# A new order for the first slots of a sparse-attention and feed-forward kernel, with 18 filler matmuls

## The chip, the cores and the metric

The kernel runs on one core of a Trainium2 chip. The metric is device microseconds of one execution. An execution of the kernel took 270.89 us (median of three, 269.55 to 270.93).

## The reference

Attention with two sparse masks, then a multiplicative feed-forward network on its output. B = 8, 8 heads, 576 rows, head width 64; 4608 tokens, model width 512, inner width 1024.

```python
scores = scale * np.matmul(q, k.transpose(0, 1, 3, 2))
mask_local = (rel >= 0) & (rel < stride)                   # heads 0..3, stride 32
mask_strided = (rel >= 0) & (pos[None, :] % stride == pos[:, None] % stride)   # heads 4..7
scores = np.where(masks, scores, -1000000000.0)
scores = scores - np.max(scores, axis=-1, keepdims=True)
attn = np.exp(scores)
attn = attn / (np.sum(attn, axis=-1, keepdims=True) + 1e-09)
x = np.matmul(attn, v)                                     # as 4608 tokens x 512
out = ((x @ w1) * (x @ w2) @ w3) @ w_out
```

## The kernel before

The work is cut into 32 *pairs*: pair i is two heads of batch i // 4. Pairs with i % 4 = 0 or 1 are local, 2 or 3 strided. The steps of a pair, with their lines:

- `load_qk` (L88): q and k from HBM to the tile `s16` (four buffers), cast to fp16 on the way, issued on GpSimd's queue: one transfer each for a local pair (L100), two each for a strided one (L105).
- `load_v` (L108): a local pair's v goes as fp32 in small pieces to one of two tiles `vsL`, three transfers on SyncE's queue (L117, L119); with `gate` a memset on VectorE comes first (L115). A strided pair's v goes as fp16 to `vhS`, four transfers on GpSimd's queue (L130).
- `emit_T` (L292): 36 or 44 transposes on TensorE (L301) into the two buffers of the PSUM pool `psA`, and the copies of q and k out of it (L309 local, L314 and L315 strided).
- `emit_S` (L319): the scores on TensorE (L333 local, L339 strided) and the addition of the mask on VectorE (L345).
- `emit_max` (L353), `emit_sub` (L360) on VectorE, `emit_exp` on ScalarE (L372), `emit_norm`: sum and reciprocal on VectorE (L380, L382), the product on GpSimd or, with `dve`, on VectorE (L383).
- `emit_P`: five or six transposes of the probabilities (L401), through `psA` too, and one copy (L404).
- `emit_cast_v` (L281): a local pair's v to fp16; `shift_v` (L289, L290): a copy of it moved by 32 rows, by two transfers on SyncE's queue.
- `emit_V`: probabilities times v (L421 local, L438 strided), copied to `xT` (L426, L442, L444, L446).

The weights w3 and w_out are folded into one matrix `wfh`. `load_w3` (L212) loads two blocks of w3 as one transfer of 512 KB (of the fp16 written), `load_wo` (L208) half of w_out, `load_w` (L205) half of w1 or w2, all on GpSimd's queue. `fold_t` (L223, L225) makes eight transposes and a copy, `fold_m` (L233, L236) four 128x512 matmuls for each of two halves and, after the second, a copy to `wfh`. The default engine of a copy in `fold_m`, `emit_P` and `emit_V` is ScalarE, in `fold_t` VectorE, in `emit_cast_v` GpSimd; in the order, `cp` is VectorE and `act` ScalarE.

The feed-forward part runs over nine chunks of 512 tokens. A piece of it is `emit_a` (L248, L252) or `emit_b` (L258, L261): four 128x512 matmuls each, a copy on ScalarE, a product on VectorE; sixteen such pieces make a chunk, then `emit_out` (L269, L274, L275) eight matmuls for each of four blocks of rows. `feed(us, batches)` emits pieces, 0.87 for one of a or b and 1.74 for an output block, until its credit is used up; nothing can be fed before x of the first 512 tokens, that is V of pairs 0 to 3, is there.

All PSUM tiles but those of `psA` come from one pool of six buffers (`psF`). Every engine works through its instructions in the order of emission, as the five queues have it. That order is written out by hand as a list of steps for the first slots, up to pair 8 or so (L504 to L674 before); then a loop (L675) goes on for pairs 9 to 31, and `feed(1e9, B)` ends it. GpSimd's transfers use eight semaphores in turn: each issue waits for the landing of the one eight issues before it. Where GpSimd's queue holds a product of `emit_norm`, all issues behind it wait as well.

`warm(n)` (L485) is n matmuls 128x512 of a zeroed tile `wz` into a `psF` buffer that nobody reads. It is defined before the change, but not called.

The stretch of the list before that matters here, shortened:

```python
zero_S(); load_v(1); load_qk(0, "k"); make_maskL(); load_qk(1, "k"); make_identity(nc, id16)
load_qk(0, "q"); load_qk(1, "q"); load_v(0, True); load_w3(2, 2)
```

Of the kernel before, what the change touches and what calls it, by code (L numbers as in the profile page):

```python
# [27 lines left out]
def kernel(  # L28
# [79 lines left out]
    def load_v(i, gate=False):  # L108

        b, hp, local, par = where(i)  # L110
        h0 = 2 * hp
        if local:
            vt = vsL[par]
            if gate:
                nc.vector.memset(vt[:, 0:LC - 1, 0, 0:1], 0.0)  # L115
            for h in range(2):
                nc.sync.dma_start(vt[:, 0:LC - 1, h, :],  # L117
                                  _ap(v[b, h0 + h], 0, [[D, P], [P * D, LC - 1], [1, D]]))
            nc.sync.dma_start(vt[0:HALF, LC - 1],  # L119
                              v[b, h0:h0 + 2, P * (LC - 1):S].rearrange("h p d -> p h d"))  # L120
        else:
            vt = att.tile([P, 2, 6 * D], FP16, tag="vhS", bufs=4, name="vhS")
            if i + 1 == 4 * B:
                nc.vector.memset(vt[HALF + 32:P, 1, 4 * D:5 * D], 0.0)
            for half in range(2):
                for h in range(2):
                    n = 6 - half
                    for r0, ap, m in strided_rows(i, h, n):
                        m = m if half else n
                        nc.gpsimd.dma_start(vt[HALF * half + r0[0]:HALF * half + r0[1], h, 0:m * D],  # L130
                                            _ap(v[b, h0 + h], 6 * half * D + ap[0],
                                                ap[1] + [[1, m * D]]))
            pts.setdefault(i, {})["v"] = vt.rearrange("p h (t d) -> p t h d", d=D)
            return
        staged[i] = vt
# [23 lines left out]
    def make_sel():  # L159
        nc.gpsimd.memset(sel, 1.0)  # L160
        for sg in (1, -1):
            nc.gpsimd.affine_select(out=sel, in_=sel, compare_op=ALU.is_ge, fill=0.0, base=0,
                                    pattern=[[0, 22], [sg, 3]], channel_multiplier=-sg)
# [43 lines left out]
    def load_wo(c):  # L207
        nc.gpsimd.dma_start(woh[:, c:c + 4, :], wor[:, c:c + 4, :])  # L208

    def load_w3(c, n=2):  # L210
        w3 = wst.tile([P, n, DF], FP16, tag="w3s", bufs=4, name="w3s")
        nc.gpsimd.dma_start(w3.rearrange("p i n -> p (i n)"), w3r[:, c // 2, :])  # L212
        for i in range(n):
            w3st[c + i] = w3[:, i, :]
# [276 lines left out]
    def zero_S():  # L491
        for t in qTS + prS:
            nc.vector.memset(t, 0.0)
# [7 lines left out]
    dve = nc.vector  # L501
    cp, act, pool = nc.vector.tensor_copy, nc.scalar.copy, nc.gpsimd.tensor_copy
    with tc.manual_schedule():
        zero_S()  # L504
        load_v(1)
        load_qk(0, "k")
        make_maskL()
        load_qk(1, "k")
        make_identity(nc, id16)
        load_qk(0, "q")  # L510
        load_qk(1, "q")
        load_v(0, True)
        load_w3(2, 2)
        load_qk(2, "k")
        load_qk(2, "q")
        make_sel()
        load_wo(0)
        load_qk(3, "k")
        zero_L(1)
        zero_L(0)  # L520
        emit_T(0, cp)
        load_w3(0, 2)
        emit_S(0)
        emit_T(1)
        load_qk(3, "q")
        emit_max(0)
        emit_cast_v(1, cp)
        nc.vector.memset(wz, 0.0)
        load_wo(4)
        make_maskS()  # L530
        load_v(3)
        emit_sub(0)
        emit_exp(0)
        emit_norm(0)
        emit_S(1)
        emit_T(2)
        fold_t(3, act)
        fold_t(2, act)
        emit_cast_v(0, cp)
        emit_max(1)  # L540
        load_w3(4, 2)
        emit_sub(1)
        load_qk(4, "k")
        emit_exp(1)
        fold_m(3, 0)
        load_qk(4, "q")
        fold_m(2, 0)
        emit_S(2)
        emit_norm(1)
        shift_v(0)  # L550
        emit_T(3)
        load_w(w1r, w1h, 0)
        load_v(2)
        fold_t(0, cp)
        fold_t(1, act)
        emit_P(0)
        emit_S(3)
        emit_max(3)
        load_w(w2r, w2h, 0)
        load_qk(5, "q")  # L560
        emit_max(2)
        fold_m(1, 0)
        shift_v(1)
        fold_m(1, 1, cp)
        fold_m(2, 1)
        load_qk(5, "k")
        emit_sub(3)
        fold_m(3, 1, cp)
        emit_sub(2)
        emit_exp(3)  # L570
        emit_norm(3)
        emit_P(1)
        fold_m(0, 0)
        emit_exp(2)
        fold_m(0, 1)
        fold_t(4, cp)
        fold_t(5, cp)
        emit_V(0)
        load_qk(6, "q")
        load_qk(6, "k")  # L580
        emit_V(1)
        emit_norm(2, dve)
        emit_T(4)
        fold_m(5, 0)
        load_w3(6, 2)
        fold_m(5, 1)
        emit_P(3)
        emit_P(2, cp)
        fold_m(4, 0)
        emit_V(2)  # L590
        emit_V(3)
        emit_S(4)
        load_qk(7, "k")
        feed(3.04, 1)
        emit_max(4)
        load_qk(7, "q")
        emit_sub(4)
        emit_T(5, cp)
        feed(2.61, 1)
        load_w(w1r, w1h, 1)  # L600
        emit_S(5)
        emit_T(6)
        emit_max(5)
        load_w(w2r, w2h, 1)
        emit_exp(4)
        fold_m(4, 1, cp)
        fold_t(6, act)
        fold_t(7, act)
        emit_sub(5)
        load_v(4, True)  # L610
        load_qk(8, "k")
        emit_T(7)
        emit_S(6)
        emit_max(6)
        fold_m(6, 0)
        fold_m(7, 0)
        emit_sub(6)
        emit_exp(6)
        emit_norm(4)
        load_qk(8, "q")  # L620
        emit_exp(5)
        load_v(5, True)
        emit_S(7)
        feed(1.46, 1)
        fold_m(6, 1)
        load_qk(9, "q")
        emit_norm(6, dve)
        emit_max(7)
        load_qk(9, "k")
        load_qk(10, "q")  # L630
        emit_cast_v(5, act)
        emit_norm(5)
        feed(0.43, 1)
        fold_m(7, 1, cp)
        emit_P(4, cp)
        emit_cast_v(4, act)
        feed(1.03, 1)
        load_v(6)
        shift_v(5)
        shift_v(4)  # L640
        load_qk(10, "k")
        load_v(8)
        load_v(10)
        feed(2.77, 1)
        emit_T(8)
        load_v(7)
        load_v(9, True)
        emit_sub(7)
        feed(2.17, 1)
        emit_P(6)  # L650
        emit_S(8)
        emit_exp(7)
        emit_norm(7, dve)
        emit_P(5, cp)
        emit_max(8)
        feed(2.17, 1)
        emit_sub(8)
        emit_T(9, cp)
        emit_V(4, cp)
        load_qk(13, "q")  # L660
        emit_V(5, cp)
        emit_exp(8)
        load_qk(12, "q")
        load_qk(11, "k")
        emit_V(6)
        emit_P(7)
        emit_cast_v(8, act)
        shift_v(8)
        load_qk(11, "q")
        emit_cast_v(9, cp)  # L670
        emit_norm(8)
        load_qk(13, "k")
        load_qk(12, "k")
        feed(3.17, 1)  # L674
        for n in range(9, NP + 2):  # L675
            full = (n - 1) // 4
            first = full - 1 if n % 4 == 1 else full
            f = 5.2
            if n < NP:
                shift_v(n)  # L680
                emit_S(n)
            if n + 1 < NP:
                emit_T(n + 1)
            if n + 5 < NP:
                load_qk(n + 5)
            for i in (n + 3, n + 2):
                if i < NP and where(i)[2] == (i == n + 3):
                    load_v(i)
            for i in (n - 3, n - 2):
                if i + (3 if by_dma(i) and i % 4 < 3 else 2) == n:  # L690
                    emit_V(i)
            if n < NP:
                emit_max(n)
            feed(0.1 * f, first)
            if n < NP:
                emit_sub(n)
                emit_exp(n)
                emit_norm(n)
                if n + 1 < NP:
                    emit_cast_v(n + 1)  # L700
            feed(0.15 * f, first)
            if n <= NP and not by_dma(n - 1):
                emit_P(n - 1)
            feed(0.55 * f, full)
            if n < NP and n % 2 == 1:
                for i in (n - 1, n):
                    if by_dma(i):
                        emit_P(i)
            feed(0.2 * f, full)
        feed(1e9, B)  # L710
# [31 lines left out]
```

## Time and profile before

| | us |
|---|---|
| median of three executions | 270.89 |
| the profiled execution | 270.49 |
| its span, first to last instruction | 268.7 |
| TensorE busy | 250.3 (93%) |
| VectorE busy | 178.4 (66%) |
| GpSimd busy | 152.7 (57%) |
| ScalarE busy | 139.1 (52%) |
| first matmul | 9.33 |
| first matmul of the feed-forward part | 36.52 |

The profile is one execution. Times in it count from the first instruction. PE is TensorE, PEld its weight loads, DVE VectorE, ACT ScalarE, POOL GpSimd, SP SyncE. A line of a timeline gives the start, the duration, engine, line and operation, the tile written and the tiles read, the count, and in brackets the engine's idle time before it and what ended it. A line of the chain of work that ended last gives the start, the duration and where the time lay. In the page's second part each digit is a slice of 6.7 us, in tenths busy.

### The profile page before, as it was taken

The page shows a single profiled execution, that of the slowest core. Times are in us where ns is not written, and L with a number is a line of the kernel's source. Part 1 is how long each engine was busy: PE and PEld are TensorE (multiplying, and loading weights), DVE is VectorE, ACT ScalarE, POOL GpSimd, SP SyncE. Part 2 cuts the span into 40 slices and gives each one's busy share as a digit, 9 for nine tenths or more (in the row PEclk, how much of TensorE's full clock was granted, in tenths as well). Part 3 has the DMA queues.
Part 4 walks back from the last instruction along what each step waited for, and adds up shares of the span by engine and source line. Part 5 has one row for each costly group of instructions (what it writes and reads, how often), then busy time and mean ns, then how long its engine had stood idle before and what let it go on. Part 6 is the DMA issues. An engine that isn't in the chain of part 4 may idle for free.

```text
span 268.7 us, 9825 instructions
## 1 busy us (share of the span) xinstructions
PE 250.3 (93%) x4186; PEld 130.3 (48%) x4186; DVE 178.4 (66%) x357; ACT 139.1 (52%) x253; POOL 152.7 (57%) x236
## 2 busy tenths in 40 slices
PE   0288999999999999999999999999999999999995
PEld 0255656455554555554555455544554444444443
DVE  3378849999778768868886787678768823432210
ACT  3254756576655664666566466546655444333322
POOL 7688673498984896489468856886683110000000
PEclk9999999999999999999999999999999999999999
DMA  6999999999999699998998998996575152002113
GB/s 123 175 209 222 194 189 164 174 162 227 190 195 169 111 225 199 113 188 185 125 155 219 194 146 77 253 177 107 82 181 102 29 111 78 2 1 78 39 60 139
DMA packets 66237, 38.75 MB, mean 144 GB/s; under 512 B 45588, under 2 KB 60944, under 8 KB 66192
## 3 DMA queue, kind: packets, MB, share of 16 engines
q0 software_dynamic: 22112, 17.29, 43.3%
q1 hardware_dynamic: 44080, 20.82, 38.5%
q8 instruction: 33, 0.54, 0.8%
q14 instruction: 12, 0.10, 0.1%
HBM read 39.24 MB, written 9.44 MB: 181 GB/s over the span
## 4 chain that ended last, share of the span: by engine, by line
PE 75%; DMA 9%; DVE 8%; POOL 3%; issue 2%; ACT 2%; POOLq 0%; DVEq 0%; ACTq 0%
PE ops L269 22%; PE aps L248 20%; PE bps L258 20%; PE fps L233 3%; DMA w3s<-in_moe_w_dram 3%; DMA s<-in_q_dram 3%; PE tpq L301 2%; DMA s<-in_k_dram 2%; PE op L421 2%; PE sp L333 2%; DVE tmp L360 2%; PE op L438 1%; DMA vhS<-in_v_dram 1%; DVE tmp L345 1%; DVE sm L380 1%
## 5 line engine op out<-in xcount | busy, mean ns | idle before, releaser
L248 PE MATMUL aps<-xT,w1h 128*128 128x512 f16 x288 | 74.1, 380 | 0.1
L258 PE MATMUL bps<-xT,w2h 128*128 128x512 f16 x288 | 73.9, 379 | 0.0
L261 DVE TENSOR_TENSOR abt<-bps,asb 128x512 f16<-128x512 f32 x72 | 47.8, 679 | 32.1 <-PE bps L258 30.1
L269 PE MATMUL ops<-wfh,abt 128*128 128x512 f16 (+1 forms) x296 | 65.6, 374 | 0.2 <-DVE xT L426 0.2
L252 ACT COPY asb<-aps 128x512 f32<-128x512 f32 x72 | 41.4, 585 | 33.3 <-PE aps L248 20.0
L130 POOL DMA_DIRECT2D vhS<-in_v_dram x70 | 43.1, 755 | 3.1 <-DMA s<-in_k_dram 1.4
L258 PEld LDWEIGHTS <-w2h 128*128 128x128 f16 x288 | 28.1, 98 | 33.5
L269 PEld LDWEIGHTS <-abt 128*128 128x128 f16 x296 | 27.8, 98 | 30.7 <-issue 0.3
L248 PEld LDWEIGHTS <-w1h 128*128 128x128 f16 x288 | 27.0, 98 | 30.8
L274 ACT COPY osb<-ops 128x512 f32<-128x512 f32 (+1 forms) x36 | 20.7, 579 | 31.6 <-PE ops L269 28.8
L383 POOL TENSOR_TENSOR prS<-prS,rc 128x594 f16<-128x594 f16 x13 | 15.4, 1183 | 29.9 <-ACT asb L252 14.4
L383 POOL TENSOR_TENSOR prL<-prL,rc 128x576 f16<-128x576 f16 x16 | 19.2, 1200 | 13.6 <-DVE vsL L115 8.4
L360 DVE TENSOR_TENSOR tmp<-tmp,mx 128x576 f32<-128x576 f32 (+1 forms) x32 | 26.1, 816 | 0.9
L301 PE MATMUL tpq<-id,s 54*64 54x54 f16 (+1 forms) x640 | 17.4, 196 | 9.6 <-DMA s<-in_q_dram 9.6
L353 DVE TENSOR_REDUCE mx<-tmp 128x9 f32<-128x576 f32 (+1 forms) x32 | 24.2, 758 | 0.5
L105 POOL DMA_DIRECT2D s<-in_q_dram x35 | 21.2, 630 | 4.9 <-PE tpk L301 2.3
L105 POOL DMA_DIRECT2D s<-in_k_dram x35 | 21.9, 686 | 2.8 <-DMA s<-in_q_dram 2.0
L372 ACT ACTIVATE prS<-tmp 128x594 f16<-128x594 f32 x16 | 11.2, 700 | 20.8 <-DVE tmp L360 14.0
L301 PEld LDWEIGHTS <-s 54*64 54x64 f16 (+1 forms) x1280 | 14.4, 112 | 12.1 <-DMA s<-in_q_dram 9.7
L380 DVE TENSOR_REDUCE sm<-prS 128x11 f32<-128x594 f16 x16 | 12.3, 770 | 9.9 <-ACT prS L372 9.9
L345 DVE TENSOR_TENSOR tmp<-sp,maskL 128x320 f32<-128x320 f32 (+1 forms) x32 | 13.1, 450 | 8.4 <-PE sp L333 8.3
L380 DVE TENSOR_REDUCE sm<-prL 128x9 f32<-128x576 f16 x16 | 12.0, 753 | 9.8 <-ACT prL L372 9.8
(78 smaller groups left out, 272.9 us busy)
## 6 DMA issues: line engine op xcount, KB each, us to landing
out_dram<-osb SPq DMA_DIRECT2D x35, 256.0 KB, 3.2
vsL<-in_v_dram SPq DMA_DIRECT2D x32, 128.0 KB, 5.2
s<-in_k_dram POOLq DMA_DIRECT2D x16, 144.0 KB, 5.0
s<-in_q_dram POOLq DMA_DIRECT2D x16, 144.0 KB, 4.2
s<-in_k_dram POOLq DMA_DIRECT2D x31, 74.2 KB, 5.1
s<-in_q_dram POOLq DMA_DIRECT2D x31, 74.2 KB, 5.4
w3s<-in_moe_w_dram POOLq DMA_DIRECT2D x4, 512.0 KB, 7.4
vhL<-vhL SPq DMA_DIRECT2D x16, 120.0 KB, 3.8
```

Of the source, the lines that this page charges most:

```text
L105: nc.gpsimd.dma_start(t[p0 + r0[0]:p0 + r0[1], h, 0:n * D], _ap(src[b, h0 + h], 0 + ap[0], ap[1] + [[1, n * D]]))
L130: nc.gpsimd.dma_start(vt[HALF * half + r0[0]:HALF * half + r0[1], h, 0:m * D], _ap(v[b, h0 + h], 6 * half * D + ap[0], ap[1] + [[1, m * D]]))
L248: nc.tensor.matmul(aps, cols(w1h, ci, jc), xT[ci][:, c * NT:(c + 1) * NT], start=(ci == 0), stop=(ci == KC1 - 1))
L252: nc.scalar.copy(out=asb, in_=aps)
L258: nc.tensor.matmul(bps, cols(w2h, ci, jc), xT[ci][:, c * NT:(c + 1) * NT], start=(ci == 0), stop=(ci == KC1 - 1))
L261: nc.vector.tensor_mul(abts[c][:, jc, :], bps, abts.pop((c, jc)))
L269: nc.tensor.matmul(ps, abts[c][:, jc, ts * P:(ts + 1) * P], wfh[:, jc, n * w:n * w + w], start=(jc == 0), stop=(jc == KC2 - 1))
L301: nc.tensor.transpose(tp[HALF * h:HALF * h + HALF, s, :], s16[p0:p0 + npar, h, s * D:(s + 1) * D], id16[p0:p0 + npar, p0:p0 + npar])
L353: nc.vector.tensor_reduce(out=mx, in_=tmp, axis=AX.X, op=ALU.max)
L360: nc.vector.tensor_tensor(out=tmp, in0=tmp, in1=_sub(mx, 0, P, 0, [[1, nt], [0, w]]), op=ALU.subtract)
L380: nc.vector.tensor_reduce(out=sm, in_=prv, axis=AX.X, op=ALU.add)
L383: eng.tensor_tensor(out=prv, in0=prv, in1=_sub(rc, 0, P, 0, [[1, nt], [0, w]]), op=ALU.mult)
```

## The change

Only the hand-written list changes; all functions are the same, and so is the loop behind it. The new front:

```diff
-        zero_S()
-        load_v(1)
-        load_qk(0, "k")
-        make_maskL()
-        load_qk(1, "k")
-        make_identity(nc, id16)
-        load_qk(0, "q")
-        load_qk(1, "q")
-        load_v(0, True)
-        load_w3(2, 2)
...
+        load_v(0)
+        nc.vector.memset(wz, 0.0)
+        warm(2)
+        zero_S()
+        load_qk(0, "q")
+        zero_L(0)
+        make_identity(nc, id16)
+        load_qk(0, "k")
+        warm(2)
+        warm(4)
+        load_v(1)
+        warm(2)
+        load_w3(2, 2)
+        load_qk(1, "k")
+        load_qk(1, "q")
+        make_maskL()
+        emit_T(0)
+        warm(1)
+        warm(1)
+        zero_L(1)
+        emit_S(0)
+        load_qk(2, "k")
+        fold_t(3, cp)
+        load_qk(2, "q")
+        load_wo(0)
+        emit_max(0)
+        make_sel()
+        warm(3)
+        emit_T(1)
+        emit_sub(0)
+        load_qk(3, "k")
+        load_qk(3, "q")
+        emit_exp(0)
+        warm(3)
+        load_w3(0, 2)
+        make_maskS()
+        emit_T(2)
+        emit_norm(0, dve)
+        fold_t(2, act)
+        emit_S(1)
+        emit_max(1)
+        emit_sub(1)
+        load_wo(4)
+        load_qk(4, "q")
+        fold_m(3, 0)
+        emit_S(2)
+        load_qk(4, "k")
```

The rest of the list, in the order of the steps that the next section speaks of (steps between them left out):

```text
before: emit_T(0, cp) ... emit_S(0), emit_T(1) ... make_maskS() ... emit_S(1), emit_T(2), fold_t(3, act),
        fold_t(2, act) ... fold_m(3, 0), fold_m(2, 0), emit_S(2), emit_norm(1), emit_T(3), fold_t(0, cp),
        fold_t(1, act), emit_P(0), emit_S(3) ... V(0) to V(3), emit_S(4), load_qk(7, "k"), feed(3.04),
        emit_max(4), emit_sub(4), emit_T(5, cp), feed(2.61) ... load_v(4, True), load_qk(8, "k"), emit_T(7),
        emit_S(6), emit_max(6), fold_m(6, 0), fold_m(7, 0), emit_sub(6), emit_exp(6), emit_norm(4),
        load_qk(8, "q"), emit_exp(5), load_v(5, True), emit_S(7), feed(1.46) ... emit_norm(6, dve) ...
        emit_cast_v(5, act) ... emit_P(4, cp), emit_cast_v(4, act) ... load_v(10), feed(2.77), emit_T(8), load_v(7)
after:  ... fold_m(2, 0), emit_sub(2), fold_t(1, act), emit_S(3), fold_t(0, act), emit_P(0, cp), four halves of
        fold_m, emit_norm(1), emit_T(4), fold_m(3, 1), emit_norm(2, dve), fold_m(0, 1), emit_norm(3),
        emit_P(1, cp), emit_P(2), emit_S(4), fold_t(5, cp), fold_t(4, act), emit_V(0, cp), emit_V(1), emit_P(3),
        three halves of fold_m, emit_V(2), emit_V(3), fold_m(5, 1), feed(2.61), emit_T(5), feed(3.04),
        emit_sub(4) ... load_v(4, True), fold_m(6, 0), emit_S(6), emit_exp(5), emit_max(6), emit_norm(4),
        load_qk(8, "k"), emit_T(7), fold_m(6, 1), load_qk(8, "q"), feed(2.17), emit_sub(6), fold_m(7, 0),
        emit_cast_v(4, act), emit_S(7), load_v(5), load_v(6), emit_cast_v(5, act), emit_exp(6), emit_P(4),
        load_qk(9), emit_norm(5), fold_m(7, 1), emit_norm(6), feed(1.03), load_qk(11, "k"), feed(2.77),
        load_qk(10, "q"), shift_v(4), emit_T(8, cp), emit_max(7), feed(2.17), emit_P(5) ... load_qk(10, "k"),
        load_v(7) ... emit_T(9, cp) ... load_v(10)
```

The sum of all credits given to `feed` in the list is the same before and after. The engines of some copies change: q's copy of T(0) and T(5) goes to ScalarE, that of T(8) to VectorE; the casts of v of pairs 0 and 9 leave VectorE for ScalarE and GpSimd; of the copies of `fold_t` VectorE has 3 and 5 (before 0, 4 and 5), of those of `fold_m` block 4 (before 1, 3, 4 and 7), of `emit_P` pairs 0, 1 and 7 (before 2, 4 and 5), of `emit_V` pair 0 (before 4 and 5); the product of `emit_norm` is on VectorE for pairs 0, 2 and 7 (before 2, 6 and 7).

More of the change, by code (lines that the diff above doesn't have):

```diff
@@ L512 @@
-        load_v(0, True)
-        load_w3(2, 2)
+        emit_T(0)
[3 more added lines that the diff above has]
+        emit_S(0)
         load_qk(2, "k")
+        fold_t(3, cp)
         load_qk(2, "q")
+        load_wo(0)
+        emit_max(0)
         make_sel()
-        load_wo(0)
+        warm(3)
+        emit_T(1)
+        emit_sub(0)
         load_qk(3, "k")
-        zero_L(1)
-        zero_L(0)
-        emit_T(0, cp)
+        load_qk(3, "q")
+        emit_exp(0)
+        warm(3)
         load_w3(0, 2)
-        emit_S(0)
@@ L524 @@
[L524 to L528, printed above, removed]
-        load_wo(4)
[L530 to L542, printed above, removed]
+        make_maskS()
+        emit_T(2)
+        emit_norm(0, dve)
@@ L543 @@
+        fold_t(2, act)
+        emit_S(1)
+        emit_max(1)
+        emit_sub(1)
+        load_wo(4)
+        load_qk(4, "q")
+        fold_m(3, 0)
+        emit_S(2)
         load_qk(4, "k")
         emit_exp(1)
-        fold_m(3, 0)
-        load_qk(4, "q")
+        load_v(3)
+        emit_T(3)
+        emit_max(2)
+        emit_cast_v(0, act)
         fold_m(2, 0)
-        emit_S(2)
-        emit_norm(1)
[L550 to L558, printed above, removed]
-        load_w(w2r, w2h, 0)
-        load_qk(5, "q")
[L561 to L565, printed above, removed]
-        load_qk(5, "k")
[L567 to L576, printed above, removed]
@@ L577 @@
-        fold_t(5, cp)
-        emit_V(0)
+        load_w3(4, 2)
+        emit_sub(2)
+        fold_t(1, act)
+        load_w(w1r, w1h, 0)
+        emit_S(3)
+        emit_cast_v(1, cp)
+        emit_max(3)
+        fold_t(0, act)
+        emit_sub(3)
+        emit_exp(2)
+        emit_P(0, cp)
+        fold_m(1, 0)
+        emit_exp(3)
+        shift_v(0)
+        fold_m(1, 1)
+        load_v(2)
+        fold_m(2, 1)
+        fold_m(0, 0)
+        emit_norm(1)
+        emit_T(4)
+        fold_m(3, 1)
@@ L579 @@
+        shift_v(1)
+        emit_norm(2, dve)
+        load_w(w2r, w2h, 0)
+        fold_m(0, 1)
+        emit_norm(3)
+        emit_P(1, cp)
+        emit_P(2)
+        emit_S(4)
+        fold_t(5, cp)
+        fold_t(4, act)
+        emit_V(0, cp)
+        load_qk(5, "q")
+        load_qk(5, "k")
         load_qk(6, "q")
+        emit_V(1)
+        emit_P(3)
+        load_w3(6, 2)
+        emit_max(4)
         load_qk(6, "k")
-        emit_V(1)
-        emit_norm(2, dve)
-        emit_T(4)
+        fold_m(4, 0)
@@ L584 @@
+        fold_m(4, 1, cp)
         fold_m(5, 0)
[L585 to L589, printed above, removed]
         emit_V(2)
         emit_V(3)
-        emit_S(4)
-        load_qk(7, "k")
+        fold_m(5, 1)
+        feed(2.61, 1)
+        emit_T(5)
         feed(3.04, 1)
-        emit_max(4)
+        emit_sub(4)
         load_qk(7, "q")
[L597 to L600, printed above, removed]
+        fold_t(6, act)
@@ L601 @@
         emit_S(5)
         emit_T(6)
+        emit_exp(4)
+        load_qk(7, "k")
+        load_w(w1r, w1h, 1)
         emit_max(5)
+        fold_t(7, act)
         load_w(w2r, w2h, 1)
[L605 to L608, printed above, removed]
         emit_sub(5)
         load_v(4, True)
+        fold_m(6, 0)
+        emit_S(6)
+        emit_exp(5)
+        emit_max(6)
+        emit_norm(4)
         load_qk(8, "k")
         emit_T(7)
-        emit_S(6)
-        emit_max(6)
@@ L615 @@
-        fold_m(6, 0)
+        fold_m(6, 1)
+        load_qk(8, "q")
+        feed(2.17, 1)
+        emit_sub(6)
         fold_m(7, 0)
-        emit_sub(6)
-        emit_exp(6)
[L619 to L625, printed above, removed]
-        load_qk(9, "q")
-        emit_norm(6, dve)
-        emit_max(7)
[L629 to L638, printed above, removed]
+        emit_cast_v(4, act)
+        emit_S(7)
+        load_v(5)
+        load_v(6)
+        emit_cast_v(5, act)
+        emit_exp(6)
+        emit_P(4)
+        load_qk(9, "q")
+        emit_norm(5)
+        load_qk(9, "k")
+        fold_m(7, 1)
+        emit_norm(6)
+        feed(1.03, 1)
+        load_qk(11, "k")
+        feed(2.77, 1)
+        load_qk(10, "q")
@@ L639 @@
+        shift_v(4)
+        emit_T(8, cp)
+        emit_max(7)
+        feed(2.17, 1)
+        emit_P(5)
         shift_v(5)
-        shift_v(4)
+        load_v(9)
+        emit_P(6)
+        emit_S(8)
         load_qk(10, "k")
         load_v(8)
-        load_v(10)
[L644 to L666, printed above, removed]
+        load_v(7)
+        emit_V(4)
+        emit_sub(7)
+        emit_max(8)
+        emit_exp(7)
+        emit_sub(8)
+        load_qk(13, "k")
+        load_qk(13, "q")
+        emit_V(5)
+        emit_exp(8)
+        emit_T(9, cp)
@@ L667 @@
+        feed(0.43, 1)
+        load_qk(11, "q")
+        feed(1.46, 1)
+        emit_norm(7, dve)
+        load_v(10)
+        emit_norm(8)
         emit_cast_v(8, act)
         shift_v(8)
[L669 to L672, printed above, removed]
+        feed(3.17, 1)
+        emit_P(7, cp)
         load_qk(12, "k")
-        feed(3.17, 1)
+        load_qk(12, "q")
+        emit_cast_v(9)
+        emit_V(6)
         for n in range(9, NP + 2):
```

## The prediction

> **What bounds the kernel now.** I read the slices of the page first, then the chain that ended last in order of time, then TensorE's timeline of the first 40 us, and last the waits of TensorE behind that.
>
> ```profile
> PE   0288999999999999999999999999999999999995
> ...
> DMA  6999999999999699998998998996575152002113
> ```
>
> From the fourth slice (20 us) to the last TensorE is full, and in the first five (to 33 us) the transfers are full too. So there are two regimes: a front that waits for data, and a body of TensorE work that only a hole can lengthen. The chain says which data:
>
> ```profile
> 5.66 7.45 DMA w3s<-in_moe_w_dram
> 13.11 0.28 issue
> 13.39 0.58 POOL w3s L212
> 13.98 0.01 issue
> 13.98 7.22 DMA s<-in_q_dram
> 21.20 0.04 issue
> 21.25 0.38 PE tpq L301 x2
> ...
> 59.31 5.61 DMA s<-in_k_dram
> 64.92 0.28 issue
> 65.20 3.74 DMA vhS<-in_v_dram
> 68.94 0.04 issue
> 68.98 0.34 PE op L438 x19
> ```
>
> Up to 21.2 us the chain lies in transfers and in GpSimd's issue of them (the transfer at 13.39 waits for the one eight issues before it). Then TensorE carries it to 43.7, VectorE to 55, GpSimd (a norm, then seven issues) and two transfers to 68.98, where V of pair 7 starts. The timeline shows what the front costs TensorE:
>
> ```profile
> 9.33 0.26 PE L301 MATMUL tpq<-id,s 64*64 64x64 f16 x2 [9.33 <-DMA s<-in_q_dram]
> ...
> 15.82 1.93 PE L223 MATMUL w3tp<-id,w3s 128*128 128x128 f16 x16
> 18.00 2.65 PE L233 MATMUL fps<-woh,w3T 128*128 128x512 f16 x8 [0.25 <-ACT w3T L225]
> ...
> 21.88 1.21 PE L223 MATMUL w3tp<-id,w3s 128*128 128x128 f16 x16
> ...
> 24.19 3.63 PE L233 MATMUL fps<-woh,w3T 128*128 128x512 f16 x16 [0.53 <-ACT w3T L225]
> ...
> 36.52 1.04 PE L248 MATMUL aps<-xT,w1h 128*128 128x512 f16 x4
> ```
>
> Sixteen 128x128 transposes took 1.93 us at 15.82 and 1.21 at 21.88; four wide matmuls at 18.00 stood 0.42 us apart, those at 24.19 0.22. TensorE runs at half its pace until about 19.5 us (the granted clock of the page says 1.00 all along and doesn't show it). At 36.52 the first matmul on xT starts. Behind it TensorE waited 1.6 us in all for other engines and transfers, five waits of 0.2 to 0.4 us.
>
> **The front, part by part.** *Loads.* Up to w2h half 0 the new order moves the same bytes; only the sequence differs. The transfers are full from 2.2 us on in before, with v of pairs 0 and 1 in small packets, and stay so; so the last of these bytes lands when it did, at 29.06 + 7.4 = 36.5 us, and each landing is found by counting bytes at before's pace. q and k of pair 0 are now GpSimd's first two (k behind the identity, 0.6 us): about 7.3 us, before 9.33. w3 rows 2 and 3 go ahead of pair 1, 368 KB after 9.33 at 174 KB/us (before: 656 KB from 9.33 to 13.11): 11.4. Pair 1: 13.1. Pair 2 (15.0) and the first woh (9.61 + 9.0 = 18.6) are as before. Pair 3 goes ahead of w3 rows 0 and 1: 20.1 instead of 21.2, and those rows 21.7 instead of 20.7. q and k of pair 4 go ahead of w3 rows 4 and 5: these about 30.2 instead of 28.8.
>
> *TensorE.* T(0) starts about 2 us earlier, and that gain is lost at once: fold_t(3) waits until 11.4, T(1) until 13.1, T(2) until 15.1, the first fold_m until 18.6, T(3) until 20.1, fold_t(1) until 21.7. Before 21.7 every step ends in a wait for a landing.
>
> *The 18 fillers.* 18 x 0.42 us = 7.6 us at the slow pace, 3.9 at the fast one. Ten stand ahead of T(0) (about 1.3 to 5.5 us), two ahead of S(0), three each ahead of T(1) and of the mask's matmul. All lie in those holes: I cost them at nothing. Without that cover the last eight cost 8 x 0.42 = 3.4 us. What they bring is the fast pace earlier: slow excess in before is 0.85 (transposes at 15.82) + 0.85 (four wide matmuls) + about 1 in the small ones = 2.7 us, but it all lies ahead of the landings at 20.7 and 21.2. I take 0; the ends are 0 and -2.7.
>
> The Trainium skill, "TensorE: Matmul & The Clock Gate", Part 1, says that the array starts at half clock, is released by some 3.4 us of sustained activity and falls back after an idle window. The rows agree on the half pace. By that rule alone the fillers would give the 2.7 us.
>
> *Mask's matmul.* In before it waited 1.9 us for VectorE's copies of sel with T(1) done and S(1) behind it. Now the exponential is issued ahead of it and sub(0) precedes sel's copies; it runs at about 14.5 us (14.11). GpSimd's two maskS steps and the second woh issue wait behind it, 0.5 us later than the 15.07 of before; the queue in front (first woh, pair 3, w3) lasts to 21.7, so 0.
>
> *From 21.7 us to the first feed.* By warm rows: ten fold_m halves x 0.865 (3.63 - 0.17, over 4) = 8.65; four fold_t x 0.54 = 2.2; S(3), S(4) 0.7; T(4) 0.42; P(0) to P(3) 1.2; V(0) to V(3) 1.15. Sum 14.3, plus 0.7 for seams (before: 11.8 of such rows took 12.4 from 24.19 to 36.59). Feed starts at 21.7 + 15.0 = 36.7, with 0.2 more for w3 rows 4 and 5: 36.9. It has one fold_m half (0.865) behind it that before did later, so TensorE is 36.52 + 0.87 - 36.9 = 0.5 us ahead. Most of it is the 0.53 us wait for ScalarE at 24.19. VectorE must deliver norm(1) to norm(3) in this stretch; by its rows (0.75 us an operation) rc of pair 1 is ready at 27.0, the product at 28.2, P(1) is due at 29.0: slack 0.8.
>
> **The middle, 37 to 69 us.** TensorE's work from feed to V(7): 16 pieces x 0.865, three output pieces x 1.73, T(5) to T(10) 2.6, S(5) to S(9) 1.8, folds 4.5, P and V 2.3 = 30.3, seams 0.7. That ends at 67.9. Two places can hold it. First, VectorE: sub(4) now stands behind three abt products, so norm(4)'s reciprocal is ready at 43.2 + 6.4 = 49.6, GpSimd's product at 50.8 (before 50.72 to 51.87). Then cast_v(4) and cast_v(5) stand on ScalarE ahead of exp(6): v of pair 4 is issued behind sub(5)'s end at 47.1, v of pair 5, which no longer waits for a memset of its own, right behind it until 49.7; it lands about 53.7 (before's last issue, 51.58, ended ScalarE's wait at 54.80: 3.2; the page's median is 5.2), exp(6) ends at 55.0, VectorE waits for it in norm(6) with three products behind. T(8)'s q copy on VectorE then ends at 59.4 and P(5), which needs its buffer, waits 0.7 us. Second, v of pair 7: norm(6) on GpSimd to 58.0, k of pair 11 issued to 59.2 and landing at 58.6 + 5.6 = 64.2, the last piece of v(7) behind it + 0.3 + 3.7 = 68.2. TensorE arrives at 67.9 + 0.7 = 68.6. Before: 68.98. **Gain 0.4 us.**
>
> *Copies moved between engines* (VectorE to ScalarE or GpSimd, net): one q copy 0.75, two casts of v 0.96, one w3T 0.66, three wfh 2.04, one half of V 0.38: VectorE loses 4.8 us of work, ScalarE gains about 4.2. I count only what the walk above uses. norm(0) goes to VectorE and norm(6) to GpSimd: 0.78 against 1.18 us, in no wait of TensorE beyond those named.
>
> One row speaks of a price there: a subtraction on VectorE (0.77 us) took 1.97 at 77.53 while GpSimd's product ran 1.20 from 77.65. The Trainium skill, "SBUF — State Buffer", section "SBUF: two separate sides", calls this an exclusive lock of a shared port pair; the row agrees, 0.77 + 1.20 = 1.97. One of 32 subtractions met it; with a norm moved to GpSimd another may, so the sum has 0 and the range 1.2.
>
> **The sum.** Behind V(7) the code is the same. Against the profiled execution: 268.7 - 0.4 = 268.3 span, plus 270.49 - 268.7 = 1.8 around it: **270.1 us**. The median of the runs shown, 270.89, lies 0.4 above that execution. A measurement of this kernel tells about 0.5% (1.35 us) from no change, so this is no change.
>
> **Rivals.**
> 1. *Slower: norm(4) holds the loads of pair 8.* In before k of pair 8 was issued at 41.65, ahead of the 8.4 us (the longest wait of GpSimd) for norm(4). Now k and q both stand behind it: reciprocal 49.6 + 1.2 + 1.2 (two issues) + 4.3 (landing) = 56.3, exactly when TensorE reaches T(8). No slack: each us by which VectorE is later there is a us on the end, decisive from 51.4 (0.4 + 1.35 over). With ScalarE's wait for v(5) in the same chain I price it at +2.5: 272.6. For it: VectorE was 6.89 of 7.00 us busy from 43 to 50. Against: its list there is 0.5 us shorter. Chance 0.28.
> 2. *Faster: VectorE's 4.8 us.* The waits at P(5), v(7) and the two of TensorE near 82 and 88 (0.4 each) go: V(7) at 67.9, -1.1 and -0.8: 268.6. Against: ScalarE's wait for v(5) remains. Chance 0.14.
> 3. *Faster: the pace of TensorE.* The 2.7 us count in full: 267.8. Against: the landings. Chance 0.06.
> 4. *The fillers don't fit* (slow pace, ahead of T(1) and T(2)): up to 1.3 us there, hidden by the first woh at 18.6; it ends as the forecast.
>
> Forecast 0.52 (269.2 to 271.6 alone). Range with the others, up to 1.2 us of a stretched subtraction included: 268.4 to 273.0. Faster by over 0.5%: 0.14 + 0.06 = 0.20; slower 0.28; within 0.52.
>
> **What would show it.** T(0) near 7.3 us and fold_t(1) near 21.7; the first feed matmul at 36 to 37.5; GpSimd's first norm behind w2h half 1 at 49.6; T(8) without a wait; V(7) at 68.6. Wrong it is if the transfers of the front end well before 36 us, or if TensorE waits over 1 us between 50 and 69.

## The result, and the profile after

The changed kernel takes **272.35 us** (median of 22 executions; 270.9 for 22 of the kernel before beside it): a ratio of 1.0049, 95% interval 1.0028 to 1.0070. It is slower by 1.3 us, about what the text on record calls the limit of a measurement, and the time lies in its range; but the forecast was 0.8 us below the kernel before's median, and the change goes the other way. A second measurement of the same kernel gave 1.0049 again (1.0022 to 1.0076). The profiled execution took 272.48 us, its span is 270.8. The page's slices first (TensorE, its granted clock, the transfers):

```profile
PE   6397999999799999999999999999999999999995
...
PEclk9687999999999999999999999999999999999999
...
DMA  6999999899999799979979997999587132001113
```

TensorE starts earlier, with fillers, and is full in the third slice (before: an 8). But the fourth (20 to 27 us) is at 7 where before had an 8, and the eleventh (67.7 to 74.5 us) is at 7 where before had a 9. (So before was full from the fifth slice on, 27 us, and not from the fourth, as the text on record reads it.) The transfers are as full as before in the first seven slices, and the clock's second to fourth digits are below 9, where before had a 9 in every slice. The chain that ended last, in order of time (start, duration, where the time lay):

```profile
3.30 9.04 DMA w3s<-in_moe_w_dram
12.39 1.07 PE w3tp L223 x8
...
18.62 0.76 DVE prL L383
19.38 0.74 DVE tmp L345 x2
20.14 0.76 DVE mx L353
...
21.61 0.83 DVE tmp L345 x2
...
22.86 1.07 PE w3tp L223 x8
24.38 1.01 PE w3tp L223 x8
```

Before, transfers and their issue carried it to 21.2 us. Now one transfer carries it to 12.4, and VectorE from 17.2 to 22.9: norm(0), which the change gives to VectorE, S(1), max(1) and S(2) stand ahead of the copy that TensorE waits for. That is this one execution, and only just: rows 0 and 1 of w3, which the same matmuls need, landed at 22.81, and the copy ended at 22.83. In ten of the eleven other profiles with the new front (all but e4, where TensorE came to this step without a wait), it is that landing that ends the wait, at 22.0 to 23.6 us. TensorE's timeline:

```profile
7.05 0.22 PE L301 MATMUL tpk<-id,s 64*64 64x64 f16 x2 [1.19 <-DMA s<-in_k_dram]
...
12.39 1.07 PE L223 MATMUL w3tp<-id,w3s 128*128 128x128 f16 x8 [3.12 <-DMA w3s<-in_moe_w_dram]
...
22.86 1.07 PE L223 MATMUL w3tp<-id,w3s 128*128 128x128 f16 x8 [1.79 <-DVE qTS L314]
...
39.14 1.03 PE L248 MATMUL aps<-xT,w1h 128*128 128x512 f16 x4
...
70.27 0.32 PE L438 MATMUL op<-pT,vhS 54*64 54x54 f16 x17
72.14 0.22 PE L438 MATMUL op<-pT,vhS 54*64 54x54 f16 x5 [1.56 <-issue]
```

The feed starts at 39.14 instead of 36.52, and 0.87 of that is the half of fold_m that was moved ahead of it: 1.75 us late. And V(7) is broken off after 17 of 22 matmuls for 1.56 us, in which TensorE waited for nothing that the profile shows.

**An account of the span.** From every trace three numbers can be read: the start of the feed (less the 0.87 where that half of fold_m stands ahead), the holes behind it (stretches of over 0.02 us in which no matmul runs on TensorE), and the rest up to the last matmul. The rest is 226.9 to 227.8 us in all twenty profiles, whatever the order. So the first two tell the kernels apart: before 36.52 and 1.52 us, after 38.28 and 2.25. These are single executions, and executions of one kernel differ by about 2 us up and down (22 of before lie between 269.0 and 273.6); the ratios, of 9 to 12 executions each (22 for the result), decide, and the profiles say where to look.

| kernel | ratio to before | 95% interval | feed | holes behind it |
|---|---|---|---|---|
| before | 1 | | 36.52 | 1.52 |
| after | 1.0049 | 1.0028 to 1.0070 | 38.28 | 2.25 |
| e17, after again | 1.0049 | 1.0022 to 1.0076 | 37.77 | 3.20 |
| e1, new front, old rest | 1.0003 | 0.9970 to 1.0036 | 37.23 | 3.20 |
| e9, e1 again | 1.0034 | 0.9999 to 1.0070 | 37.30 | 3.17 |
| e2, old front, new rest | 1.0067 | 1.0027 to 1.0107 | 36.27 | 3.03 |
| e10, e2 again | 1.0061 | 1.0030 to 1.0092 | 36.57 | 2.22 |
| e3, after without fillers | 1.0031 | 1.0001 to 1.0061 | 38.12 | 2.73 |
| e8, before with fillers | 1.0042 | 1.0010 to 1.0073 | 36.38 | 1.02 |
| e4, w3 behind pair 1 | 1.0078 | 1.0045 to 1.0112 | 37.80 | 1.77 |
| e11, early shifts | 1.0072 | 1.0038 to 1.0105 | 37.31 | 3.24 |
| e5, norm(8) ahead of v(10) | 1.0039 | 1.0012 to 1.0067 | 38.14 | 1.76 |
| e6, v(7) ahead of k(11) | 1.0034 | 1.0005 to 1.0062 | 36.40 | 2.91 |
| e7, exp(6) ahead of casts | 1.0039 | 1.0001 to 1.0078 | 37.30 | 1.09 |
| e12, e2 with the three mends | 1.0022 | 0.9990 to 1.0053 | 37.63 | 4.21 |
| e15, e12 again | 1.0048 | 1.0012 to 1.0083 | 37.47 | 3.43 |
| e13, after with the three mends | 1.0011 | 0.9978 to 1.0045 | 38.37 | 4.57 |
| e18, e13 again | 1.0024 | 0.9987 to 1.0061 | 36.54 | 2.81 |
| e14, before with two places | 1.0003 | 0.9973 to 1.0032 | 36.67 | 2.83 |
| e16, e2 with old engines | 1.0077 | 1.0035 to 1.0118 | 37.17 | 2.71 |

The profiled executions of e12 and e13 were disturbed (274.1 and 275.7 us), so the means below leave them out.

### The profile page after: what moved, and what is told of

Same layout as the page of the kernel before. It is cut to its first block, busy times and chain, and to the rows that moved or that the text cites. A ratio compares the mean times of both kernels' runs of the same rounds, so it can differ in the third digit from the quotient of the medians.

```text
span 270.8 us, 9863 instructions
## 1 busy us (share of the span) xinstructions
PE 257.1 (95%) x4204; PEld 132.5 (49%) x4204; DVE 174.4 (64%) x346; ACT 143.3 (53%) x260; POOL 153.0 (57%) x237
## 4 chain that ended last, share of the span: by engine, by line
PE 78%; DVE 7%; DMA 7%; POOL 3%; issue 3%; ACT 1%; DVEq 0%; POOLq 0%; ACTq 0%
PE ops L269 23%; PE aps L248 20%; PE bps L258 19%; PE fps L233 3%; DMA w3s<-in_moe_w_dram 3%; PE tpq L301 3%; PE op L421 2%; PE w3tp L223 2%; DMA s<-in_k_dram 2%; PE sp L333 2%; DMA vhS<-in_v_dram 2%; PE op L438 2%; DVE mx L353 1%; DVE tmp L345 1%; PE sp L339 1%
## 5 line engine op out<-in xcount | busy, mean ns | idle before, releaser
L383 POOL TENSOR_TENSOR prS<-prS,rc 128x594 f16<-128x594 f16 x14 | 16.7, 1191 | 30.7 <-ACT asb L252 14.4
L383 POOL TENSOR_TENSOR prL<-prL,rc 128x576 f16<-128x576 f16 x15 | 18.6, 1237 | 11.5 <-PE aps L248 6.9
L105 POOL DMA_DIRECT2D s<-in_q_dram x35 | 21.2, 634 | 5.1 <-PE tpk L301 2.2
L105 POOL DMA_DIRECT2D s<-in_k_dram x35 | 21.7, 676 | 3.9 <-DMA w3s<-in_moe_w_dram 2.3
L301 PE MATMUL tpk<-id,s 54*64 54x54 f16 (+1 forms) x640 | 16.7, 194 | 1.3 <-DMA s<-in_k_dram 1.2
L301 PE MATMUL tpq<-id,s 54*64 54x54 f16 (+1 forms) x640 | 17.2, 193 | 0.0
```

The costliest lines, as they stand in the source:

```text
L105: nc.gpsimd.dma_start(t[p0 + r0[0]:p0 + r0[1], h, 0:n * D], _ap(src[b, h0 + h], 0 + ap[0], ap[1] + [[1, n * D]]))
L301: nc.tensor.transpose(tp[HALF * h:HALF * h + HALF, s, :], s16[p0:p0 + npar, h, s * D:(s + 1) * D], id16[p0:p0 + npar, p0:p0 + npar])
L383: eng.tensor_tensor(out=prv, in0=prv, in1=_sub(rc, 0, P, 0, [[1, nt], [0, w]]), op=ALU.mult)
```

## The experiments

### The two halves of the list (e1, e2, e9, e10)

The list is cut where the feed begins. Theory: the front costs the time, since its feed starts later. Rival: the rest does.

```diff
 e1, e9: the new list to fold_m(5, 1), then of the old list:
-feed(2.61, 1)
...
+load_qk(7, "k")
+feed(3.04, 1)
...
 e2, e10: the old list to emit_S(4), then of the new list:
-load_qk(7, "k")
-feed(3.04, 1)
...
+emit_max(4)
+fold_m(4, 1, cp)
+feed(2.61, 1)
...
```

> The new list up to V of pair 3, then the old list from the first feed on (max of pair 4 and fold_m(4, 1), which the new front already holds, are left out of it). Theory A, the front lost it (its feed began at 39.14 us, 1.75 late for its work) and the middle only passes it on: about +1.3 us on before, ratio 1.005, and V of pair 7 near 71. Theory C, the middle lost it (1.56 us of waiting inside V of pair 7): ratio 1.000, V of pair 7 near 69 as GpSimd's old order sends its v earlier.

> The old list up to S of pair 4, max of pair 4 and fold_m(4, 1), then the new list from the first feed on. Theory A: ratio 1.000 or a little under it, feed near 37.4 us. Theory C: the +1.3 us stays, ratio 1.005, with a wait of 1 us or more inside V of pair 7 though the feed begins on time.

> The same kernel as the first of the two hybrids (new list up to V of pair 3, old list from the first feed on), measured a second time since its interval of 0.997 to 1.0036 leaves a loss of 0.35% open and its one profile had the feed 1.6 us late. Theory T, the list behind the first feed is what lost: again 1.000, within 0.002. Theory A, the front: 1.003 to 1.006.

> The same kernel as the second hybrid (old list up to the first feed, new list behind it), measured a second time. Theory T: again 1.005 or more. Theory A: 1.000 to 1.002. Both near 1.003 would mean that each half carries a part.

Measured: 1.0003 and 1.0034 with the new front alone, 1.0067 and 1.0061 with the new rest alone. The theory falls: the rest by itself costs as much as the whole change (both intervals lie above 1), and the front by itself less, some 0.2%, not told from nothing. Yet its delay is there: the feed starts at 37.47 us in the mean of the profiles with the new front or a variant of it (11, from 36.40 to 38.28) and at 36.72 with the old one (7, from 36.27 to 37.47). That is 0.75 us, by their spread 0.2 to 1.3, or 0.1 to 0.5% of the time. The wait of over 1 us inside V(7) that was expected with the new rest alone didn't come: V(7) runs whole in both. e2 has a hole of 0.77 us further on, in front of a feed-forward piece, and e10 one of 0.77 at P(8), for norm(8).

### Parts of the new front (e3, e8, e4, e11)

```diff
 e3 (all seven calls of warm go; the memset stays)
-        warm(2)
...
 e8, in the old list: the memset first, then the fillers ahead of T(0), S(0), T(1) and the mask's matmul
+        nc.vector.memset(wz, 0.0)
+        warm(2)
...
 e4, in the new list
-        load_w3(2, 2)
         load_qk(1, "k")
         load_qk(1, "q")
+        load_w3(2, 2)
         make_maskL()
 e11, in the new list (the same four steps go from behind S(3), P(0) and T(4))
+        emit_cast_v(0, act)
+        shift_v(0)
         emit_T(1)
         emit_sub(0)
+        emit_cast_v(1, cp)
+        shift_v(1)
```

> The new list without its 18 fillers. Theory B, fillers at the slow pace stand in front of T(1), T(2) and what hangs on them: faster than the changed kernel by 0.5 to 1.3 us, ratio 0.999 to 1.003 to before. Theory A: fillers lie in waits for landings, so it ends as the changed kernel does, ratio 1.004 to 1.007, first feed at 39 us within 0.5. If the fast pace that they bring was worth anything, it is slower than the changed kernel.

> The old list with the 18 fillers added at the same steps (ten ahead of T(0), two ahead of S(0), three ahead of T(1), three ahead of the mask's matmul) and the zeroing of their tile first. Theory A and my prediction's step on fillers: they lie in holes and what they speed up waits for landings; ratio 1.000, within 0.002, first feed at 36.5 us within 0.7. The rule of the clock: the slow pace of 14 to 19.5 us goes, feed up to 2.7 us earlier, ratio 0.990 to 0.997. Theory B, fillers in the way: 1.002 or more.

> The new list with the first load of w3 put behind q and k of pair 1, as in the old one; nothing else. Theory A in its first form (that load of 512 KB pushed pair 1 and all behind it): T(1) near 11 us instead of 14.6, VectorE's chain 2 to 3 us earlier, feed 1 us or more earlier, ratio 1.000 to 1.002 to before. If only the total of bytes counts: T(1) earlier, but fold_t(3) later, feed at 39 us, ratio 1.004 to 1.006.

> The new list with the casts of v of pairs 0 and 1 and the shifts on SyncE's queue moved forward, ahead of T(1) and behind sub(0), so that these four transfers run beside the front's big loads at 10 to 18 us as in the old list and not at 24 to 30. If the front's bytes land late because GpSimd's queue runs alone in 12 to 24 us (186 GB/s against 209): feed up to 1 us earlier, w2h half 0 landing near 37 instead of 38.4, ratio 1.002 to 1.004. If not: feed at 38 to 39 us, ratio 1.004 to 1.006.

*Fillers.* Without them the new list measures 1.0031, with them 1.0049: not told apart. The old list with them has its feed at 36.38, where it was at 36.52, and measures 1.0042. So they bring the feed nothing in either list. Whether they cost something is open: the interval of the old list with them (1.0010 to 1.0073) lies above 1, where 1.000 within 0.002 was expected, though its one profile is the shortest of all (269.5 us); and the new list is not slower without them. Nor do they hold the clock. This is after in stretches of 2 us (length, busy us and count of TensorE, weight loads, VectorE, ScalarE, GpSimd; granted clock, mean DMA load, GB/s):

```profile
10.00:12.00 2.00, 0.00 (x0) 0.00 (x0) 0.22 (x1) 0.00 (x0) 0.37 (x1) 0.50 1.16 195
...
22.00:24.00 2.00, 1.15 (x20) 0.97 (x24) 1.97 (x5) 1.61 (x4) 0.57 (x1) 0.68 1.02 186
24.00:26.00 2.00, 2.00 (x36) 1.81 (x33) 1.81 (x5) 1.55 (x2) 0.00 (x0) 0.50 1.27 186
```

The third column from the right is the clock: 0.50 in the hole of 3.1 us that ends at 12.4, and again behind the hole of 1.8 us that ends at 22.86, so that the two fold_t there took 1.07 and 1.08 us (0.65 to 0.72 in the eleven other profiles with the new front). In the second profile of after (e17) it was 1.00 from 22 to 26, and the feed came at 38.6 all the same.

*Order of the loads.* Neither w3 behind pair 1 nor the shifts of v earlier helps: 1.0078 and 1.0072. Both are slower than before, and not told from after. In e4, T(1) started at 15.10 us, where 11 was expected and after has 14.68: in TensorE's order fold_t(3) still stands ahead of it, and w3 now landed at 12.8. So e4 doesn't tell what w3 ahead of pair 1 costs by itself. In e11 the transfers did move 211 GB/s from 12 to 24 us (after 186), but only 186 from 24 to 36 (after 201), and the landing at the end of the front came no earlier (38.98). So the late shifts alone don't make the front late.

### Three places in the rest (e5, e6, e7, e12 to e15, e17, e18)

Theory: V(7) broken off for 1.56 us is the wait for v of pair 7, which k of pair 11 now precedes; P(8) and others wait for norm(8), which v of pair 10 precedes on GpSimd; ScalarE's casts hold exp(6). Rival: many small things, or something else.

```diff
 e5
+        emit_norm(8)
         load_v(10)
-        emit_norm(8)
 e6
+        load_v(7)
         load_qk(11, "k")
...
-        load_v(7)
 e7
+        emit_exp(6)
         emit_cast_v(4, act)
...
-        emit_exp(6)
```

> The new list with norm(8) put ahead of v of pair 10, so that GpSimd's product for P(8) no longer stands behind four issues that wait for v of pair 7 to land. Theory D, the queue of GpSimd around pairs 7 and 8 is what the new list lost (TensorE stood 1.6 us there in the changed kernel, 1.9 without fillers, 0.8 with the old front, 0.4 before): ratio 1.000 to 1.002 to before, no wait of P(8) for the product. Theory A, the front: it stays at 1.004 to 1.006.

> The new list with v of pair 7 put ahead of k of pair 11 and q and k of pair 10 on GpSimd's queue: issued about 3.5 us earlier, at 60 us instead of 63.5. Theory D: the wait inside V of pair 7 (1.56 us) goes, and the four issues of v of pair 10 wait less; ratio 1.000 to 1.002. If T(10) then waits for k of pair 10, the loss only moves: ratio 1.004 to 1.006 with a wait in T(10). Theory A: 1.004 to 1.006 without one.

> The new list with the exponential of pair 6 put ahead of the casts of v of pairs 4 and 5 on ScalarE, which wait 1.1 and 1.0 us for their transfers there. The chain that I walked in the prediction (exp(6), norm(6), GpSimd's queue, v of pair 7): exp(6) 2 to 3 us earlier, norm(6) 1 us earlier at most since GpSimd is busy until 59 us, ratio 1.001 to 1.004. If that chain is not what holds the end: 1.004 to 1.006.

1.0039, 1.0034, 1.0039: none of the three alone brings the kernel back, and none is told from 1.0049. In e5 the hole in V(7) is 1.35 us; in e6 and e7 there is none, though e7 changes nothing about v of pair 7. Then all three mends, behind the old front (e12, e15) and in the whole new list (e13, e18), and, the other way, two of the places put into the old list:

```diff
 e14, in the old list
+        load_qk(11, "k")
         load_v(7)
...
-        load_qk(11, "k")
...
+        load_v(10)
         emit_norm(8)
```

> The second hybrid with three mends in its new half at once: norm(8) ahead of v of pair 10, v of pair 7 ahead of k of pair 11, the exponential of pair 6 ahead of the casts of pairs 4 and 5. Theory T with GpSimd's queue as its place: 1.000 to 1.002. If the loss of the new half lies in something else (which copies ScalarE has, loads of pair 8 behind norm(4)): 1.004 or more.

> The new list with all three places mended: norm(8) ahead of v of pair 10, v of pair 7 ahead of k of pair 11, exp(6) ahead of the casts of pairs 4 and 5. If these places carry the loss of the half behind the first feed, only the front's 0.0 to 0.3% is left: ratio to before 1.000 to 1.003. If the loss lies in many small things, the single mends (1.0034 to 1.0039) already gave what there is: 1.003 to 1.005.

> The old list with two places of the new one put in: k of pair 11 is loaded ahead of v of pair 7, and v of pair 10 directly ahead of norm(8). If the places carry the loss, V(7) waits over 1 us in the trace and the ratio is 1.003 or more. If they don't, 1.000 with the interval's 0.3% around it.

> The kernel of the twelfth run once more (old front, new half behind the first feed with the three mends; 1.0022, which is told from neither 1.000 nor 1.005). If the places carry the loss: 1.000 to 1.003. If not: about 1.006, as without the mends.

> The changed kernel once more, beside the mended one. All theories: 1.003 to 1.007.

> The new list with the three mends once more. If the three places carry the larger part of the loss: 0.999 to 1.003, and at least 0.3% under the unmended list beside it. If the loss is spread over many things: 1.003 to 1.006, and within 0.2% of the unmended list beside it.

1.0022 and 1.0048 behind the old front; 1.0011 and 1.0024 in the whole list, where after beside it had 1.0049. Beside after that is 0.25% less, between what the two theories expected; 1.0011 alone would fit the first theory. The intervals overlap: the mends may be worth half of the loss, and no single pair of runs proves it. The two places in the old list cost nothing that shows (1.0003, up to 0.3% by its interval), against the theory. But in e14's profile a hole of 1.39 us stands, not in V(7), but in the middle of the six transposes of a P, where nothing is waited for:

```profile
PE pp L401 <- issue: 1.4, 1, 1.4
PE pp L401 <- POOL prL L383: 0.6, 1, 0.6
```

### The engines of the copies (e16)

e2 with the copies of T(5), T(8), P(4), P(5), P(7), V(4), V(5), fold_m(7, 1), the cast of pair 9 and the product of norm(6) where they were before.

```diff
-        emit_T(5)
+        emit_T(5, cp)
...
-        emit_norm(6)
+        emit_norm(6, dve)
```

> Old front, new order behind the first feed, but copies of T(5), T(8), P(4), P(5), P(7), V(4), V(5), fold_m(7,1), the cast of pair 9 and the product of norm(6) on the engines that they had before. If the moved copies carry the loss of that half (ScalarE has about 4 us more): 1.000 to 1.003. If the order carries it: 1.005 to 1.007, as with the new engines (1.0067, 1.0061).

1.0077, as slow as with the new engines: the loss stays with the order, and these engines carry none of it that shows.

### What the hole in V(7) is

This was not tried by an experiment of its own; the traces of all the kernels tell it. The page lists a queue that no step of the kernel issues to (packets, MB, share):

```profile
q8 instruction: 33, 0.54, 0.8%
```

These are 33 packets of 16,384 bytes. TensorE has 8449 records in after (4204 matmuls, 4204 weight loads, 41 others) and 8413 in before: about 33 blocks of 256. Take TensorE's records in order of their start, in all twenty profiles, and every hole of over 0.3 us from 9 us on. In 15 of these holes, in fourteen profiles, the first instruction behind the hole waits for no semaphore, and **all fifteen stand at record 193 + 256 n**: eleven at 2497 (e1, e2, e5, e9, e11, e12, e13, e15, e16, e17 and after; in e16 it is a weight load, and the matmul behind it waits for a semaphore that was set 0.13 us before), one at 2241 = 2497 - 256 (e14), one at 3521 = 2497 + 4 x 256 (e18), two at 449 and 1729 (e6). In a sixteenth hole at such a place, 449 in e8, there is a semaphore as well. At every other hole there is one. And in all sixteen the engine goes on 1.1 to 1.7 us behind the end of the queue's packet for that block. The other boundaries say the same: with packets and blocks taken in order, the twenty profiles have 640 boundaries, and TensorE crosses none of them less than 1.1 us behind the end of its packet. Four of the sixteen:

| profile | block before entered | packet | block before used up | next starts | hole |
|---|---|---|---|---|---|
| after | 68.13 | 68.99 to 70.65 | 70.58 | 72.14 | 1.56 |
| e17 | 68.92 | 70.06 to 71.14 | 71.38 | 72.31 | 0.93 |
| e14 | 64.72 | 65.25 to 66.21 | 66.28 | 67.67 | 1.39 |
| e18 | 93.10 | 96.79 to 97.75 | 97.30 | 99.11 | 1.80 |

So TensorE ran out of instructions. In after P(7), V(6), S(9), T(10) and V(7) stand in one row, 6 + 22 + 36 + 44 + 22 short matmuls with as many weight loads, and 256 records pass in 2.3 us (in the body, where wide matmuls prevail, in about 6.4). In the sixteen the packet starts 0.5 to 4.5 us after TensorE enters the block before, takes 0.9 to 1.9, and what it brings runs 1.1 to 1.7 later. The Trainium skill, "Runtime: NRT & Kernel Launch", section "Instruction fetch mechanics", says that instructions come in blocks of 16 KiB, the next one fetched while the current one runs, and that this is mostly hidden. The trace agrees on the blocks; here it is not hidden, and the holes are 0.4 to 1.9 us long.

In e18 the hole is in a feed-forward piece, behind S, T and two V in a row, in the loop that the change leaves as it was:

```profile
PE bps L258 <- issue: 1.8, 1, 1.8
```

What it does to the median is not settled. In before the row T(9), V(4), V(5), V(6) uses up a block in 1.3 us from 63.80 on; its packet came at 62.7, ahead of the row, and there is no hole. In e14 the packet for the same block came at 65.25, behind the row's start at 64.72. What decides this is open. e14 has the hole in its profile and a ratio of 1.0003; e3, e4, e7 and e10 have none and ratios of 1.0031 to 1.0078. In the eleven profiles with the new rest and at most one mend the holes behind the feed are 2.45 us in the mean (before 1.52, e8 1.02), 0.70 of it at block boundaries. But the five with the old rest (before, e8, e1, e9, e14) have 2.35 in the mean, from 1.02 to 3.20, and 0.55 at boundaries. So the holes of single executions don't tell the two rests apart, and that the hole in V(7) is what makes the new rest slower is not shown.

## Why the prediction was wrong

- **"the last of these bytes lands when it did, at 36.5 us"**: this step failed. They landed at 38.44; in all twelve profiles with the new front at 37.57 to 39.01, in all eight with the old one at 35.67 to 37.25. The transfers were as full by the page, but slower: from 2 to 36 us after moved 6205 KB and before 6500, a packet of 4096 bytes took 364 ns instead of 339 (640 of them on 16 engines: 1.0 us). What makes them slower is open; with the shifts early (e11) it was 6347 KB and 343 ns, and the feed at 37.31 in the table. This last landing holds up nothing itself (the feed waits for TensorE's own work); the one that does is that of w3 rows 0 and 1, next.
- **The landings of the front.** T(0) at 7.3: 7.05. Pair 3 at 20.1: 19.37. w3 rows 2 and 3 at 11.4: 12.35. Rows 0 and 1 at 21.7: they landed at 22.81, and at 22.03 to 23.57 in ten of the other profiles with the new front (in e4 at 21.04, but fold_t(1) came at 23.12). In after, VectorE's copy ended 0.02 us behind the landing, so that VectorE is the last of the chain there; the text had no such wait.
- **Fillers at nothing.** Right for the gain: e3 and e8 show no move of the feed, and the rival of the full 2.7 us is out. For the cost it is open: e8 measures 1.0042 where nothing was expected, and e3 is not told from after.
- **15.0 us from there to the feed.** 16.28, from 22.86 to 39.14: 1.1 of the excess is two fold_t at 1.07 where 0.54 was taken, which the eleven other profiles don't have: that part is this one execution's luck. The feed at 36.9 came at 39.14. Of that 2.24, 1.16 are from the start of this stretch and 1.28 from its length, less 0.2 that the text had added for w3 rows 4 and 5.
- **The middle.** From the feed to V(7) 31.0 us were forecast, and 31.13 passed (before 31.91, with one half of fold_m more: 31.04; there V(7) began at 68.43 with three matmuls, and went on at 68.98, where the text has it start). norm(4) on GpSimd at 49.6 ran at 52.12, 2.5 us later, with the feed 2.24 late, and T(8) had no wait: rival 1's mechanism didn't come, and the slower side came by another. P(5)'s 0.7 us didn't come either.
- **V(7) at 68.6 and the gain of 0.4.** This step failed too, and by the ratios it weighs more: with the old front, where these bytes land as before, the new rest alone measures 1.0067 and 1.0061, a loss of 1.7 us, where the text has the middle lose 0.1 of the 0.5 that the front was ahead. In after, V(7) started at 70.27 and was broken off for 1.56. The text looked for a transfer there; the instruction stream was not among its resources at all, so its cost stood at nothing without a reason. The waits of before that rival 2 counted on did go: without this hole the holes from the feed to 110 us are 0.25 us in after, 1.19 in before.
- **The sum.** Forecast -0.4 us; the profile has +2.1: 1.76 at the feed, 0.73 in holes behind it, -0.38 in the rest. Over many profiles the feed's part is 0.75. In the ratios the rest has the larger part (0.6%), the front the smaller (0.2%), and together they measure less than their sum. Which steps of the rest make its 0.6% stays open: not the copies' engines as far as e16 tells, perhaps in part the three places, perhaps the row of short matmuls, which no run broke up. That the time came out within the stated range is no credit to the sum: the slower side of the range was there for rival 1, which didn't happen.

## What to carry to other kernels

A front in which every step waits for a landing gained nothing here by an earlier start, and the sum of bytes over a rate read from another order was no bound: the same bytes landed 2 us later in another sequence. Where short matmuls stand in a row, count them: a block of 256 instructions that is used up in some 2 us left TensorE without instructions for over 1 us in several executions here. Wide matmuls between such steps would make a block last longer; no run here tried it. A hole in the middle of one step, in front of an instruction that waits for no semaphore, is the sign of it.

## What was not expected of the hardware

- TensorE stops at the boundary of a block of 256 instructions, 0.4 to 1.9 us, in 14 of 20 profiles (in a fifteenth, e8, a semaphore stands there too); in the one of before it doesn't.
- In one execution of after the granted clock fell to 0.50 again behind a hole of 1.8 us at 22.86 us, though the last fillers had ended at 16.4, and in before's record it stands at 1.00 while wide matmuls are 0.42 us apart.
- The rest of the work behind the feed, holes left out, is the same to 0.4% over all orders (226.9 to 227.8 us): what these orders changed is the feed's start and the holes.
